# Weights loaded as f32 through a staging buffer and cast on VectorE, with wave 1 in exact order, in a fused attention and MLP kernel

## The chip, the cores and the metric

The kernel runs on one core of one Trainium2 chip. The metric is the device time of one execution in microseconds (us), as the median of several executions.

Names used below: PE is TensorE, DVE is VectorE, ACT is ScalarE, POOL is GpSimd, SP is the engine whose queue ("the sync queue") starts most DMAs. "PEclk" is the granted clock of TensorE as a share of full speed.

## The reference

A decayed linear attention over 768 positions (4 batches, 8 heads, head dimension 64) feeds an MLP of 3072 tokens, 512 to 2048 to 512:

```python
def _attn_ref(q, k, v, lam):                    # (4, 8, 768, 64), lam per head
    ...
    for b in range(nb):                         # blocks of 64 positions
        qb, kb, vb = (q[:, :, sl], k[:, :, sl], v[:, :, sl])
        intra = np.einsum('bhic,bhjc->bhij', qb, kb) * Dmask[None]
        intra = np.einsum('bhij,bhjd->bhid', intra, vb)
        inter = np.einsum('bhid,bhde->bhie', qb * lam_pow[None], kv_state)
        out[:, :, sl] = intra + inter
        kv_state = lam_block * kv_state + np.einsum('bhsd,bhse->bhde', kb * rev_pow, vb)   # cut
    return out

def _moe_ref(x, w_in, w_out):                   # x: the attention's output, (3072, 512)
    h = x @ w_in                                # w_in (512, 2048) f32
    g = h * (1.0 / (1.0 + np.exp(-1.702 * h)))
    return g @ w_out                            # w_out (2048, 512) f32
```

## The kernel before

The kernel works in six waves of 128 positions by 4 batches (512 tokens each). Wave w's attention must be done before wave w's MLP. TensorE gets one long list of work ("main": the MLP's matmuls), and the attention of the next wave ("side") is put in at chosen places of that list. All loads of q, k and v, all DMA transposes and all stores go through the sync queue, in the order of the program. All matmuls are in bf16. The weights lie in DRAM as f32, and GpSimd's DMA queue casts them on the way:

```python
    const = ctx.enter_context(tc.tile_pool(name="const", bufs=1))
    ld = ctx.enter_context(tc.tile_pool(name="ld", bufs=2))       # q, k, v as f32
    ...
    gp = ctx.enter_context(tc.tile_pool(name="gp", bufs=2))       # GELU outputs, one per wave
    op = ctx.enter_context(tc.tile_pool(name="op", bufs=4))       # output rows
    ...
    w_in_sb = [const.tile([P, KC, c * P], bf16, name=f"w_in{j}") for j, c in enumerate(IN_COLS)]     # 4 chunks
    w_out_sb = [const.tile([P, CW, d_model], bf16, name=f"w_out{j}") for j in range(FFC // CW)]      # 4 chunks

    def load_w_in(j, k0=0, k1=KC):
        f0 = sum(IN_COLS[:j]) * P
        nc.gpsimd.dma_start(
            out=w_in_sb[j][:, k0:k1, :],
            in_=moe_w_in.rearrange("(kc ki) f -> ki kc f", ki=P)[:, k0:k1, f0 : f0 + IN_COLS[j] * P])
    ... # load_w_out likewise

    behind = const.tile([1, 2], bf16)            # 4 bytes a partition

    def sync_behind(x):                          # the sync queue waits here until x has landed
        nc.sync.dma_start(out=behind, in_=x[0:1, 0, 0:2])
```

At the end of wave 0's attention it issues all weights, makes the sync queue wait for w_out's second chunk, and then issues wave 1's loads:

```python
        for j in range(1, len(IN_COLS)):
            load_w_in(j)
        for j in range(NJ):
            load_w_out(j)
        sync_behind(w_out_sb[1])
        for u in UNITS:                          # 8 units: 4 batches x 2 groups of heads
            for nm in "kqv":
                load_unit(1, nm, *u)
        nc.gpsimd.memset(v_sb[1][:, :, :, 1, :], 0.0)
        nc.gpsimd.memset(kv_sb[0], 0.0)
```

Wave 2 and later use a second form of attention, whose inputs and outputs are transposed by DMAs on the sync queue. The last of these transposes (xs to xT) is what the wave's MLP starts from:

```python
    def p_cast(w, p):
        ... # scale k and q into kqs (VectorE)
        nc.sync.dma_start_transpose(out=kq_of[w, p]..., in_=kqs...)
    def p_out(w, p):
        ... # matmuls into o
        xs = work.tile([P, B, P], bf16, tag="xs", bufs=2, name="xs")
        nc.scalar.copy(xs, o)
        nc.sync.dma_start_transpose(out=xT(w)[:, p], in_=xs.rearrange("p b c -> p (b c)"))
```

## Time and profile before

| | before |
|---|---|
| median of 4 executions (range) | 223.06 us (222.56 to 224.4) |
| TensorE busy | 208.3 us of 222.9 us |
| VectorE busy | 92.0 us, none of it from 19.5 to 39.6 us |
| first MLP matmul | 19.5 us |
| MLP of wave 1, 2, 3 begins | 56.2, 96.1, 128.2 us |
| TensorE's idle stretches over 0.15 us, after 15 us, added up | 7.4 us |

The busy table of the page of before (engine, busy us, share of the span, instructions):

```profile
span 222.9 us, 3886 instructions
...
PE 208.3 (93%) x1476; PEld 109.0 (49%) x1476; DVE 92.0 (41%) x218; ACT 95.1 (43%) x202; POOL 35.9 (16%) x57
```

TensorE bounds the kernel: only 15 us of the span are not its own. Where those 15 us lie is seen when the span is cut into stretches. Busy time in stretches of before (the first line names the columns; DMA share is that of the 16 engines, and exceeds 1 where records of packets overlap):

```profile
core 0: us, PE busy (x) PEld busy (x) DVE busy (x) ACT busy (x) POOL busy (x), PEclk, DMA share, GB/s
...
19.50:39.60 20.10, 19.76 (x94) 8.78 (x94) 0.00 (x0) 10.23 (x19) 4.62 (x5) 1.00 1.21 205
39.60:46.20 6.60, 4.38 (x22) 1.67 (x22) 1.88 (x4) 1.40 (x3) 2.09 (x4) 0.74 0.87 195
46.20:57.70 11.50, 11.50 (x98) 6.45 (x95) 6.42 (x20) 6.11 (x15) 3.19 (x6) 1.00 1.03 231
57.70:96.10 38.40, 35.18 (x341) 23.76 (x341) 24.99 (x64) 16.09 (x43) 4.05 (x7) 1.00 0.84 200
96.10:215.90 119.80, 119.80 (x771) 57.69 (x770) 45.57 (x103) 44.96 (x76) 7.85 (x9) 1.00 0.58 134
```

Read it by rows. From 96.1 us TensorE is never idle, so nothing can be won there. In the second row it is idle for 2.2 us, and the row's mean clock is 0.74. VectorE does nothing at all in the first row.

TensorE's timeline of before (start us, duration, engine, line, tiles, count; in brackets the idle time before, and what ended it):

```profile
19.52 1.04 PE L358 MATMUL ps_h<-xT,w_in 128*128 128x512 bf16 x4 [1.19 <-DMA w_in<-in_moe_w_in_dram]
...
41.56 0.28 PE L227 MATMUL ps_t<-ident,kqs 128*128 128x128 bf16 x2 [1.94 <-DVE kqs L206]
...
88.78 0.22 PE L337 MATMUL ps_o<-kv,kq 128*128 128x128 bf16 x1 [1.60 <-ACT xs L342]
```

These are the three waits that the change is aimed at: the first weights, wave 1's first block (its loads were held back by the weights), and the end of wave 2's attention.

### The profile page before, as it was taken

Reading aid. Unit: us, or ns where it says so; the run is one execution under the profiler, and the core shown is the slowest. Engines: PE = TensorE matmul, PEld = TensorE weight load, DVE = VectorE, ACT = ScalarE, POOL = GpSimd, SP = SyncE. Lnnn points to the kernel's source line nnn. Section 1 sums busy time; section 2 is a strip of 40 time slices with the busy share of each in tenths; the row PEclk is TensorE's granted clock in tenths of the full one; section 3 lists DMA queues with packets and bytes.
Section 4 is the critical chain, followed back from the end, with each engine's and each line's share of the span. In section 5 each row is a group of like instructions: output and inputs, shape, how many; then the busy total and the mean of one; then the engine's idle time right before and its main releaser. Section 6 shows DMA issues by size and latency. Waiting matters only on the chain.

```text
span 222.9 us, 3886 instructions
## 1 busy us (share of the span) xinstructions
PE 208.3 (93%) x1476; PEld 109.0 (49%) x1476; DVE 92.0 (41%) x218; ACT 95.1 (43%) x202; POOL 35.9 (16%) x57
## 2 busy tenths in 40 slices
PE   7687999699899987999999999999999999999993
PEld 2354344145784675444555444554444545444452
DVE  0792000246588984163654183572372432100121
ACT  5996662244771344146522056612076421366000
POOL 4879300232211001011020120110120000000000
PEclk9999999889999999999999999999999999999999
DMA  6999999899988797889774999747793122200112
GB/s 136 245 206 148 205 206 219 189 232 234 222 187 268 170 238 159 184 222 195 174 167 131 225 239 196 163 109 192 177 252 75 26 84 80 94 3 0 47 47 94
DMA packets 109638, 35.91 MB, mean 161 GB/s; under 512 B 102324, under 2 KB 106676, under 8 KB 109620
## 3 DMA queue, kind: packets, MB, share of 16 engines
q1 hardware_dynamic: 105236, 31.47, 60.7%
q0 software_dynamic: 4240, 4.19, 11.8%
q8 instruction: 11, 0.18, 0.4%
q14 instruction: 7, 0.06, 0.1%
q10 hardware_dynamic: 144, 0.00, 0.0%
HBM read 27.27 MB, written 6.29 MB: 151 GB/s over the span
## 4 chain that ended last, share of the span: by engine, by line
PE 74%; DMA 13%; SPq 4%; POOL 3%; DVE 3%; issue 1%; ACT 0%; DVEq 0%; ACTq 0%
PE ps_out L379 34%; PE ps_h L358 29%; DMA w_out<-in_moe_w_out_dram 7%; DMA qf<-in_q_dram 4%; SPq L82 4%; DMA xT<-xs 2%; PE ps_s L311 2%; POOL w_in L161 2%; PE ps_o L337 2%; PE ps_out L397 2%; PE ps_o L339 2%; PE ps_kv L326 2%; POOL kqs L206 1%; PE ps_t L227 1%; PE ps_s L246 1%
## 5 line engine op out<-in xcount | busy, mean ns | idle before, releaser
L358 PE MATMUL ps_h<-xT,w_in 128*128 128x512 bf16 (+1 forms) x448 | 88.5, 349 | 1.5 <-DMA w_in<-in_moe_w_in_dram 1.5
L379 PE MATMUL ps_out<-w_out,g_sb 128*128 128x512 bf16 x368 | 86.0, 384 | 0.0
L364 ACT ACTIVATE g_sb<-ps_h 128x512 bf16<-128x512 f32 (+1 forms) x112 | 59.5, 537 | 60.2 <-PE ps_h L358 59.2
L358 PEld LDWEIGHTS <-w_in 128*128 128x128 bf16 x448 | 42.1, 98 | 38.9 <-DMA w_in<-in_moe_w_in_dram 2.2
L379 PEld LDWEIGHTS <-g_sb 128*128 128x128 bf16 x368 | 34.5, 98 | 37.9 <-issue 1.0
L386 DVE COPY o_sb<-ps_out 128x512 f32<-128x512 f32 x19 | 13.1, 691 | 56.8 <-PE ps_out L379 50.2
L318 DVE TENSOR_TENSOR sm<-ps_s,dmask 128x512 bf16<-128x512 f32 x32 | 20.6, 686 | 26.9 <-PE ps_s L311 26.9
L300 POOL CAST v_sb<-vf 128x512 bf16<-128x512 f32 x16 | 12.3, 767 | 100.1 <-DMA vf<-in_v_dram 90.4
L342 ACT CAST xs<-ps_o 128x512 bf16<-128x512 f32 x16 | 9.4, 586 | 25.6 <-PE ps_o L339 23.2
L206 DVE TENSOR_TENSOR kqs<-kf,k_pow 128x256 bf16<-128x256 f32 x16 | 7.5, 469 | 27.6 <-DMA kf<-in_k_dram 23.3
L206 POOL TENSOR_TENSOR kqs<-qf,q_pow 128x256 bf16<-128x256 f32 x16 | 10.2, 641 | 29.4 <-DMA qf<-in_q_dram 26.6
L251 DVE TENSOR_TENSOR sm<-ps_s,dmask 128x512 bf16<-128x512 f32 x16 | 11.1, 691 | 5.3 <-PE ps_s L246 4.8
L329 DVE SCALAR_TENSOR_TENSOR kv<-kv,blk_pow,ps_kv 64x256 bf16<-64x256 bf16 x24 | 11.4, 476 | 0.2
L337 PE MATMUL ps_o<-kv,kq 128*128 128x128 bf16 x64 | 9.0, 220 | 1.6 <-ACT xs L342 1.6
L289 ACT CAST xT<-ps_o 128x256 bf16<-128x256 f32 x16 | 6.0, 375 | 9.7 <-PE ps_o L287 9.5
L298 DVE TENSOR_SCALAR kqs<-kf,k_pow 128x256 bf16<-128x256 f32 x32 | 9.8, 349 | 0.2
L298 DVE TENSOR_SCALAR kqs<-qf,q_pow 128x256 bf16<-128x256 f32 x32 | 9.8, 348 | 0.0
L274 DVE SCALAR_TENSOR_TENSOR kv<-kv,blk_pow,ps_kv 64x64 bf16<-64x64 bf16 x32 | 7.7, 279 | 4.9 <-PE ps_kv L262 4.5
L227 PE MATMUL ps_t<-ident,kqs 128*128 128x128 bf16 x64 | 6.8, 220 | 3.2 <-DVE kqs L206 2.5
L339 PEld LDWEIGHTS <-sm 128*128 128x128 bf16 x128 | 7.9, 98 | 3.2 <-issue 1.8
L211 ACT CAST v_sb<-vf 128x256 bf16<-128x256 f32 x16 | 6.4, 401 | 7.1 <-DMA vf<-in_v_dram 6.9
L339 PE MATMUL ps_o<-v_sb,sm 128*128 128x64 bf16 x128 | 9.0, 193 | 0.0
(54 smaller groups left out, 111.7 us busy)
## 6 DMA issues: line engine op xcount, KB each, us to landing
kf<-in_k_dram SPq DMA_DIRECT2D x48, 128.0 KB, 2.9
qf<-in_q_dram SPq DMA_DIRECT2D x48, 128.0 KB, 3.0
vf<-in_v_dram SPq DMA_DIRECT2D x48, 128.0 KB, 3.0
out_dram<-o_sb SPq DMA_DIRECT2D x23, 256.0 KB, 2.7
w_out<-in_moe_w_out_dram POOLq DMA_DIRECT2D x4, 512.0 KB, 15.8
w_in<-in_moe_w_in_dram POOLq DMA_DIRECT2D x3, 512.0 KB, 9.4
w_in<-in_moe_w_in_dram POOLq DMA_DIRECT2D x2, 256.0 KB, 5.6
kq<-kqs SPq DMA_TRANSPOSE x16, 3.5
```

Of the source, the lines that this page charges most:

```text
L206: eng.tensor_tensor(out.rearrange("s p h d -> s (p h) d"), xf.rearrange("s p h d -> s (p h) d"), tab, op=MUL)
L251: nc.vector.tensor_tensor(sm, s_ps.pop((w, b, g)).rearrange("s h (p t) -> s h p t", t=P)[:, :, 0:2, :], dmask[:, :, gs(g), :], op=MUL)
L298: nc.vector.tensor_scalar(kqs[:, i, :, h, :], loaded[w, "kq"[i], p][:, :, h, :], scalar1=(k_pow, q_pow)[i][:, 2 * p + h : 2 * p + h + 1], ...
L300: nc.gpsimd.tensor_copy(v_sb[w % 2][:, p, :, 0:3:2, :], loaded[w, "v", p])
L318: nc.vector.tensor_tensor(sm[:, h], s[:, h], dmask[:, h, p : p + 1, :].to_broadcast([P, B, P]), op=MUL)
L329: nc.vector.scalar_tensor_tensor(new[hd(h), p, :, hd(h)], old[hd(h), p, :, hd(h)], blk_pow[hd(h), 2 * p + h : 2 * p + h + 1], t[hd(h), :, ...
L337: nc.tensor.matmul(o[:, b, :], kq_of[w, p][:, 1, b, :], kv_sb[w % 2][:, p, b, :], start=True, stop=True)
L339: nc.tensor.matmul(o[:, b, hd(h)], sm[:, h, b, :], v_sb[w % 2][:, p, b, 2 * h, :], start=False, stop=True, skip_group_check=True)
L358: nc.tensor.matmul(t[:, bs[0] * P : bs[1] * P], w_in_sb[j][:, kc, i * P : (i + 1) * P], xT(w)[:, kc, bs[0] : bs[1], :].rearrange("p b t -> ...
L364: nc.scalar.activation(g_tile(w)[:, fc, c], h_ps.pop((w, fc))[:, c], GELU)
L379: nc.tensor.matmul(t, g_of[w][:, fc, g * P : (g + 1) * P], w_out_sb[j][:, fc % CW, :], start=(fc == 0), stop=(fc == FFC - 1))
L386: nc.vector.tensor_copy(o, t)
```

## The change

Its intent: take the weights off GpSimd's software queue, so that they and wave 1's loads lie in one queue in exactly the order in which they are needed; cast on VectorE, which is idle there; need no new memory, since the second GELU buffer is not used before wave 1. The weights come as 16 halves of chunks (512 KB of f32 each) through four staging slots. The places of wave 1's and wave 2's attention in the list are set anew as well. The diff, cut:

```diff
-    def load_w_in(j, k0=0, k1=KC):
-        nc.gpsimd.dma_start(...)                # and load_w_out
-    behind = const.tile([1, 2], bf16)
-    def sync_behind(x): ...
+    NS = 4
+    stage = gp.tile([P, NS, 2, W], f32, tag="g", name="w_st")
+    def load_w(kind, j, h):                     # slot = running number % NS
+        ...
+        nc.sync.dma_start(out=stage[:, slot_of[kind, j, h]], in_=src)
+    def cast_w(kind, j, h, eng, rs=slice(0, 2), cs=slice(0, W)):
+        ...
+            eng.tensor_copy(out, x)
 ...
     with tc.manual_schedule():
+        for j in range(2):
+            for h in range(2):
+                load_w("in", j, h)              # behind wave 0's loads
 ... (in wave 0's attention)
-            if i == N - 2:
-                load_w_in(0, 0, 2)
-            if i == N - 1:
-                load_w_in(0, 2, 4)
-        for j in range(1, len(IN_COLS)): load_w_in(j)
-        for j in range(NJ): load_w_out(j)
-        sync_behind(w_out_sb[1])
-        for u in UNITS: ...                     # wave 1's loads
+            if i == N:
+                for h in range(2):
+                    cast_w("in", 0, h, nc.gpsimd, slice(0, 1))
+                    cast_w("in", 0, h, nc.vector, slice(1, 2))
+        for h in range(2):
+            load_w("in", 2, h)
+        for j in range(1, NJ):
+            ...                                 # cast w_in[j], then load the next half into its slot
+        nc.gpsimd.memset(v_sb[1][:, :, :, 1, :], 0.0)
+        nc.gpsimd.memset(kv_sb[0], 0.0)
+        for j in range(2):
+            for h in range(2):
+                cast_out(j, h)
+                load_w("out", j + 2, h)
+            if j == 0:
+                for nm in "kqv":
+                    load_unit(1, nm, *UNITS[0]) # wave 1's first block, ahead of w_out's last halves
+        for u in UNITS[1:]: ...                 # the rest of wave 1's loads
 ... (order of the work; main and side now have times of their own)
-        units1(e + BOFF, UNITS[4:], BSTEP)      # BOFF, BSTEP = 4, 3.8
+        units1(e + B_AT, UNITS[4:], B_STEP, nc.scalar)   # 1, 2.5; ScalarE now copies all the turned (transposed) q and k
-                m = e - FFC - NJ * G if w > 1 else m1 - 8
-                full(m + 1, m + 10, w + 1, 3.0)          # wave 2's attention, then the later waves'
+        full(e + 8, e + 15, 2, 2.9, 3.0)                 # wave 2's attention
+        load_spread(e + 9, 3, 2)                         # wave 3's loads, amid it
```

More of the change, by code (lines that the diff above doesn't have):

```diff
@@ L154 @@
     CW = 4
+    NJ = FFC // CW
     w_in_sb = [const.tile([P, KC, c * P], bf16, name=f"w_in{j}") for j, c in enumerate(IN_COLS)]
@@ L157, with cast_out @@
     in_of = [(j, i) for j, c in enumerate(IN_COLS) for i in range(c)]
-    def load_w_in(j, k0=0, k1=KC):
-        f0 = sum(IN_COLS[:j]) * P
-        nc.gpsimd.dma_start(
-            out=w_in_sb[j][:, k0:k1, :],
-            in_=moe_w_in.rearrange("(kc ki) f -> ki kc f", ki=P)[:, k0:k1, f0 : f0 + IN_COLS[j] * P])
-    def load_w_out(j):
-        nc.gpsimd.dma_start(
-            out=w_out_sb[j],
-            in_=moe_w_out.rearrange("(fc fi) d -> fi fc d", fi=P)[:, j * CW : (j + 1) * CW, :])
-    behind = const.tile([1, 2], bf16)
-    def sync_behind(x):
-        nc.sync.dma_start(out=behind, in_=x[0:1, 0, 0:2])
-    def pow_table(pw, n, c0):
-        return pw[:, c0 : c0 + n]
+    NS = 4
+    stage = gp.tile([P, NS, 2, W], f32, tag="g", name="w_st")
+    slot_of = {}
+    def load_w(kind, j, h):
+        if (kind, j, h) not in slot_of:
+            slot_of[kind, j, h] = len(slot_of) % NS
+        if kind == "in":
+            src = moe_w_in.rearrange("(kc ki) f -> ki kc f", ki=P)[:, 2 * h : 2 * h + 2, j * W : (j + 1) * W]
+        else:
+            f = j * CW + 2 * h
+            src = moe_w_out.rearrange("(fc fi) d -> fi fc d", fi=P)[:, f : f + 2, :]
+        nc.sync.dma_start(out=stage[:, slot_of[kind, j, h]], in_=src)
+    def cast_w(kind, j, h, eng, rs=slice(0, 2), cs=slice(0, W)):
+        out = (w_in_sb if kind == "in" else w_out_sb)[j][:, 2 * h + rs.start : 2 * h + rs.stop, cs]
+        x = stage[:, slot_of[kind, j, h], rs, cs]
+        if eng is nc.scalar:
+            nc.scalar.copy(out, x)
+        else:
+            eng.tensor_copy(out, x)
+    def cast_out(j, h, eng=nc.vector):
+        for r in range(2):
+            cast_w("out", j, h, eng, slice(r, r + 1))
     x_of, g_of, h_ps, o_ps = {}, {}, {}, {}
@@ L407, in mlp2_last @@
                 nc.sync.dma_start(out=out[r0 : r0 + P, hw:], in_=o)
-    NJ = FFC // CW
     FILL0, FILL1 = 12, 1
-    BOFF, BSTEP = 4, 3.8
+    B_AT, B_STEP = 1, 2.5
     with tc.manual_schedule():
+        for j in range(2):
+            for h in range(2):
+                load_w("in", j, h)
         fill(FILL0)
@@ L456 @@
                 u_kv_up(0, *u2)
-            if i == N - 2:
-                load_w_in(0, 0, 2)
-            if i == N - 1:
-                load_w_in(0, 2, 4)
-        for j in range(1, len(IN_COLS)):
-            load_w_in(j)
-        for j in range(NJ):
-            load_w_out(j)
-        sync_behind(w_out_sb[1])
-        for u in UNITS:
+            if i == N:
[5 more added lines that the diff above has]
+        for j in range(1, NJ):
+            for c in range(2):
+                for h in range(2):
+                    cast_w("in", j, h, nc.vector, cs=slice(2 * c * P, 2 * (c + 1) * P))
+            for h in range(2):
+                if j + 2 < NJ:
+                    load_w("in", j + 2, h)
+                else:
+                    load_w("out", j + 2 - NJ, h)
+        nc.gpsimd.memset(v_sb[1][:, :, :, 1, :], 0.0)
+        nc.gpsimd.memset(kv_sb[0], 0.0)
+        for j in range(2):
+            for h in range(2):
+                cast_out(j, h)
[3 more added lines that the diff above has]
+                    load_unit(1, nm, *UNITS[0])
+        for u in UNITS[1:]:
             for nm in "kqv":
                 load_unit(1, nm, *u)
-        nc.gpsimd.memset(v_sb[1][:, :, :, 1, :], 0.0)
-        nc.gpsimd.memset(kv_sb[0], 0.0)
         for fc in range(3):
@@ L474, with put, at, units1 @@
             gelu(0, fc)
-        main = [(fc_whole, 0, fc) for fc in range(3, FFC)]
-        main += [(mlp2, 0, g, j) for j in range(NJ) for g in range(3)] + [(mlp2, 0, 3, j) for j in range(NJ)]
-        side = []
-        def units1(at, units, step):
+        main, side = [], []
+        clock = [0.0]
+        def put(length, *item):
+            main.append((clock[0], item))
+            clock[0] += length
+        def at(t, *item):
+            side.append((t, item))
+        def units1(t0, units, step, copier):
@@ L481, in units1 @@
             n = len(units)
             for i in range(n + 2):
-                t = at + step * i
+                t = t0 + step * i
+                h = t + 0.5 * step
                 if i < n:
-                    side.append((t, (u_cast_kq, 1, 0, *units[i], nc.vector)))
-                    side.append((t, (u_cast_kq, 1, 1, *units[i], nc.gpsimd)))
-                    side.append((t, (u_cast_v, 1, *units[i], nc.scalar)))
+                    at(t, u_cast_kq, 1, 0, *units[i], nc.vector)
+                    at(t, u_cast_kq, 1, 1, *units[i], nc.gpsimd)
+                    at(t, u_cast_v, 1, *units[i], nc.scalar)
@@ L488, in units1 @@
                 if 0 < i <= n:
-                    side.append((t, (u_score, 1, *units[i - 1])))
+                    at(t, u_score, 1, *units[i - 1])
+                    at(t, u_mask, 1, *units[i - 1])
                 if i < n:
-                    side.append((t + 0.5 * step, (u_turn, 1, 0, *units[i])))
-                    side.append((t + 0.5 * step, (u_turn, 1, 1, *units[i])))
-                if 0 < i <= n:
-                    side.append((t + 0.5 * step, (u_mask, 1, *units[i - 1])))
+                    at(h, u_turn, 1, 0, *units[i])
@@ L495, in units1 @@
+                    at(h, u_turn, 1, 1, *units[i])
                 if i < n:
-                    side.append((t + 0.5 * step, (u_turn_copy, 1, *units[i], nc.scalar if units[i][0] < 2 else nc.vector)))
+                    at(h, u_turn_copy, 1, *units[i], copier)
                 if i > 1:
-                    side.append((t + 0.5 * step, (u_out, 1, *units[i - 2])))
-                    side.append((t + 0.5 * step, (u_kv, 1, *units[i - 2])))
-                    side.append((t + 0.5 * step, (u_kv_up, 1, *units[i - 2])))
@@ L502 @@
-        e = len(main)
-        units1(e - 11, UNITS[:4], 2)
-        main += [(mlp1, 1, fc, [0, 1], HALF[0]) for fc in range(3)]
-        main += [(fc_rest, 1, fc, HALF[0]) for fc in range(3)]
-        main += [(fc_whole, 1, fc, HALF[0]) for fc in range(3, FFC)]
-        main += [(mlp2, 1, g, j) for g in range(2) for j in range(NJ)]
-        units1(e + BOFF, UNITS[4:], BSTEP)
-        main += [(fc_whole, 1, fc, HALF[1]) for fc in range(FFC)]
-        main += [(mlp2, 1, g, j) for g in range(2, G) for j in range(NJ)]
@@ L511, with full @@
-        m1 = e + FFC + 3 + 2 * NJ
-        side.append((13, (load_full, 2)))
-        def full(at_c, at, w, step):
+                    at(h, u_out, 1, *units[i - 2])
+                    at(h, u_kv, 1, *units[i - 2])
+                    at(h, u_kv_up, 1, *units[i - 2])
+        def full(t_cast, t0, w, step, c_step=2.0):
             for p in range(NP):
-                side.append((at_c + 2.0 * p, (p_cast, w, p)))
+                at(t_cast + c_step * p, p_cast, w, p)
             for p in range(NP + 1):
-                t = at + step * p
+                t = t0 + step * p
@@ L519, in full @@
                 if p < NP:
-                    side.append((t, (p_score, w, p)))
-                    side.append((t, (p_mask, w, p)))
-                    side.append((t, (p_kv, w, p)))
+                    at(t, p_score, w, p)
+                    at(t, p_mask, w, p)
+                    at(t, p_kv, w, p)
                 if p:
-                    side.append((t + 0.5 * step, (p_out, w, p - 1)))
-        for w in range(1, NW):
-            e = len(main)
-            if w + 1 < NW:
-                m = e - FFC - NJ * G if w > 1 else m1 - 8
-                full(m + 1, m + 10, w + 1, 3.0)
-                if w + 2 < NW:
-                    for p in range(NP):
-                        for i, nm in enumerate("kqv"):
-                            side.append((m + 4 + 2.4 * (3 * p + i), (load_pair, w + 2, nm, p)))
-                main += [(fc_whole, w + 1, fc) for fc in range(FFC)]
-                if w + 2 < NW:
-                    main += [(mlp2, w + 1, g, j) for g in range(G) for j in range(NJ)]
-                else:
-                    main += [(mlp2, w + 1, g, j) for g in range(G - 1) for j in range(NJ)]
-                    main += [(mlp2_last, w + 1, G - 1)]
+                    at(t + 0.5 * step, p_out, w, p - 1)
@@ new lines, in load_spread @@
+        def load_spread(t0, w, step):
+            for p in range(NP):
+                for i, nm in enumerate("kqv"):
+                    at(t0 + step * (3 * p + i), load_pair, w, nm, p)
+        for fc in range(3, FFC):
+            put(1, fc_whole, 0, fc)
+        for t, j, h in ((15, 2, 0), (15.5, 2, 1), (18.5, 3, 0), (20.2, 3, 1)):
+            at(t, cast_out, j, h)
+        for j in range(NJ):
+            for g in range(3):
+                put(1, mlp2, 0, g, j)
+        for j in range(NJ):
+            put(1, mlp2, 0, 3, j)
@@ new lines @@
+        at(13, load_full, 2)
+        e = clock[0]
+        units1(e - 11, UNITS[:4], 2, nc.scalar)
+        units1(e + B_AT, UNITS[4:], B_STEP, nc.scalar)
+        for fc in range(3):
+            put(0.25, mlp1, 1, fc, [0, 1], HALF[0])
+        for fc in range(3):
+            put(0.25, fc_rest, 1, fc, HALF[0])
+        for fc in range(3, FFC):
+            put(0.5, fc_whole, 1, fc, HALF[0])
+        for g in range(2):
+            for j in range(NJ):
+                put(1, mlp2, 1, g, j)
+        for fc in range(FFC):
+            put(0.5, fc_whole, 1, fc, HALF[1])
@@ new lines @@
+        for g in range(2, G):
+            for j in range(NJ):
+                put(1, mlp2, 1, g, j)
+        full(e + 8, e + 15, 2, 2.9, 3.0)
+        load_spread(e + 9, 3, 2)
+        for w in range(2, NW):
+            e = clock[0]
+            if w + 1 < NW:
+                full(e + 1, e + 10, w + 1, 3.0)
+            if w + 2 < NW:
+                load_spread(e + 4, w + 2, 2.4)
+            for fc in range(FFC):
+                put(1, fc_whole, w, fc)
+            for g in range(G - (w + 1 == NW)):
+                for j in range(NJ):
+                    put(1, mlp2, w, g, j)
@@ L541 @@
+        put(4, mlp2_last, NW - 1, G - 1)
         side.sort(key=lambda x: x[0])
-        for i, (f, *args) in enumerate(main):
-            while side and side[0][0] <= i:
+        for t, (f, *args) in main:
+            while side and side[0][0] <= t:
                 _, (g_, *b_) = side.pop(0)
```

## The prediction

> **What bounds the kernel now.** TensorE. The profile's busy table gives it 208.3 of 222.9 us. By stage (busy time in stretches of the span) it is never idle from 96.1 us, where wave 2's MLP starts, to 215.9; that stretch keeps its order of work and should not move. Time to win lies before 96.1 us:
>
> 1. Start of the first MLP: the timeline shows the first w_in matmul at 19.5 us, 1.2 us after attention's last one, waiting for w_in; another 0.3 us at 23.9.
> 2. Between 39.6 and 42.2 us: 2.2 us idle, waiting for wave 1's first block. The weights' software queue fills the DMA engines (share 1.2 from 19.5 to 39.6 us); wave 1's loads are held until w_out's second chunk lands at 34.05 us, then take 6 us instead of 3.
> 3. Then a granted clock of 0.74 (39.6 to 46.2 us): eight matmuls take 3.5 us in place of 1.7; with the attention pieces about 2.2 us lost.[...]
> 4. End of wave 1: 0.56 us at 57.7 (VectorE), 1.05 us at 78 to 79 (VectorE late with sm and kv), 1.6 us at 87 (transposing DMA, then ACT). 3.2 us.
>
> Sum: 9 us.
>
> **What the change does.** It removes 9 software DMAs and the wait for w_out; it adds 16 f32 loads of 512 KB on the sync queue through four staging slots, and their casts. Reading stays 8.4 MB. The software queue moved 206 GB/s of bf16, so it read about 412; output stores with the same 2 KB rows reach 330 to 420 GB/s in short slices. Estimate: 1.3 to 1.6 us per half chunk, so the weights are all in at 34 to 39 us. TensorE needs a new chunk each 3.5 us (in) or 2.6 us (out): enough.
>
> Casts: VectorE does 256 f32 elements in 0.349 us, so 512 in at most 0.7; 1024 per half, at most 22 us in all[...]. VectorE is idle 22.5 us there: off the path.
>
> **On the critical path.** Item 1: first weights at 17.5 to 18.5 plus one cast, win 0.5 to 1.2 us. Items 2 and 3: wave 1's first block is issued around 29 to 33 us and lands before TensorE wants it at about 37; win about 4.2 us, clock 1.0. Item 4: wave 2's attention is spread over more of wave 1's MLP; win 2 of 3.2. Given back, about 1 us: ACT now does all turn copies beside the half GELUs, VectorE is nearly full, and wave 2's last transposes leave only about 3 us of slack.
>
> **Predicted: 216.8 us**, 8 in 10 between 214.3 and 220.0. Faster by over 2%: 0.78; within 2%: 0.19; slower: 0.03.
>
> **Right if:** first w_in matmul before 19 us; no idle near 40 us and no clock under 0.95 after the start; [...]wave 2's MLP starts at 89 to 91 us; from there 126.8 us to the end.
>
> **Wrong if:** a half chunk takes 1.8 us or more (TensorE waits for w_out casts at 35 to 40 us); the in-order sync queue blocks wave 1's loads behind a slot; ACT delays GELUs around 55 to 65 us; the transposes before wave 2 end late.

The four items come to 9 us, of which 0.5 to 1.2, about 4.2 and 2 us were to be won and about 1 us given back, and 223.06 us less these 5.7 to 6.4 us are 216.7 to 217.4 us.

## The result, and the profile after

| | before | after |
|---|---|---|
| median of 4 executions (range) | 223.06 us (222.56 to 224.4) | 231.75 us (230.78 to 232.53) |
| ratio after to before, with 95% interval | | 1.0377 (1.0317 to 1.0437) |
| first MLP matmul | 19.5 us | 21.5 us |
| first w_out matmul | 34.3 us | 37.2 us |
| MLP of wave 1, 2, 3 begins | 56.2, 96.1, 128.2 us | 60.6, 99.8, 136.4 us |
| TensorE's idle stretches over 0.15 us, after 15 us, added up | 7.4 us | 10.9 us |
| span of the profiled execution | 222.9 us | 230.8 us |

A ratio here and below is the mean time of one kernel's fast runs over that of the other's in the same rounds, so it is not quite the ratio of the medians. Executions over 1.5% slower than the fastest of the same kernel are left out of the means. The kernel is slower by 3.8%, and the result was correct, as in every run below.

The busy table of the page of after:

```profile
span 230.8 us, 3923 instructions
...
PE 212.7 (92%) x1476; PEld 110.1 (48%) x1476; DVE 102.6 (44%) x244; ACT 97.0 (42%) x206; POOL 30.3 (13%) x50
```

The matmuls are the same 1476, but they are busy 4.4 us longer. Most of that is a clock, not work. Busy time in the same stretches of after:

```profile
19.50:39.60 20.10, 18.10 (x82) 8.19 (x82) 8.98 (x21) 11.14 (x23) 4.65 (x4) 0.92 0.83 283
39.60:46.20 6.60, 4.78 (x22) 1.82 (x20) 2.55 (x7) 0.99 (x2) 0.61 (x1) 0.91 1.09 339
46.20:57.70 11.50, 10.08 (x72) 4.49 (x72) 7.16 (x19) 4.99 (x11) 3.09 (x5) 0.90 1.09 212
```

In the first row 82 matmuls were done in place of 94, and although four staging slots were to keep the queue full, the DMA share is 0.83. In the second row TensorE is still idle for 1.8 us (2.2 us in before), and in the third row for 1.4 us, where before has none.

Stretches around the lower clock in after show three periods, where before had one:

```profile
19.00:26.00 7.00, 4.94 (x24) 2.19 (x22) 3.19 (x6) 2.91 (x10) 4.65 (x4) 0.76 0.91 329
42.00:50.00 8.00, 5.07 (x21) 1.40 (x19) 2.79 (x7) 0.99 (x2) 0.97 (x2) 0.79 1.06 262
...
98.00:107.00 9.00, 6.19 (x22) 2.35 (x21) 5.17 (x17) 1.21 (x3) 0.76 (x2) 0.81 0.88 211
```

Multiply what is missing to 1 by the length: 7.00 x 0.24, 8.00 x 0.21 and 9.00 x 0.19 are each 1.7 us, which is one period of 3.41 us at half clock: the trace of after has a clock of 0.50 from 21.09 to 24.50, from 44.98 to 48.39 and from 103.01 to 106.42 us. Before has 6.60 x 0.26 = 1.7 us, once (0.50 from 42.45 to 45.86 us). This is not only the profiled execution: of after's four executions three had a mean clock of 0.977 or 0.978 over the span, which is three such periods, and one had 0.990. Of the 32 executions of before in the later jobs, 19 had a clock of 0.997 or more and took 223.66 us on average; the other 13 (0.985 to 0.992; three of them slow) took 225.01 us. TensorE's timeline of after names the waits:

```profile
21.52 1.89 PE L367 MATMUL ps_h<-xT,w_in 128*128 128x512 bf16 x4 [2.00 <-POOL w_in L181]
...
43.90 0.29 PE L236 MATMUL ps_t<-ident,kqs 128*128 128x128 bf16 x2 [1.32 <-DVE kqs L215]
...
49.55 0.28 PE L236 MATMUL ps_t<-ident,kqs 128*128 128x128 bf16 x2 [0.94 <-DVE kqs L215]
...
80.45 0.40 PE L320 MATMUL ps_s<-kq 64*128 64x128 bf16 x8 [2.02 <-DMA kq<-kqs]
103.55 1.86 PE L367 MATMUL ps_h<-xT,w_in 128*128 128x512 bf16 x4 [2.71 <-DMA xT<-xs]
```

So of the loss of 7.9 us between the two profiles, 3.5 us are more idle time (10.9 less 7.4), and two more periods of half clock make at most 3.4 us (less where TensorE waits anyway): at most 6.9 us. Of the rest, 0.8 us lie before 19.5 us, where the same 126 matmuls were busy for 14.97 us in place of 14.20. What made the waits is the question. Four things are seen in the trace.

**Staging slots.** VectorE's timeline of after shows the casts waiting for halves that have not landed:

```profile
20.57 0.43 DVE L181 CAST w_in<-w_st 128x512 bf16<-128x512 f32 x1 [1.37 <-DMA w_st<-in_moe_w_in_dram]
...
24.61 2.41 DVE L181 CAST w_in<-w_st 128x512 bf16<-128x512 f32 x4 [0.61 <-DMA w_st<-in_moe_w_in_dram]
...
31.71 0.43 DVE L181 CAST w_in<-w_st 128x512 bf16<-128x512 f32 x1 [2.59 <-DMA w_st<-in_moe_w_in_dram]
...
47.10 0.76 DVE L181 CAST w_out<-w_st 128x512 bf16<-128x512 f32 x2 [3.26 <-DMA w_st<-in_moe_w_out_dram]
```

The trace gives the landing of the first four halves, which were issued together, as 20.55, 21.91, 23.24 and 24.59 us, so 1.35 us apart; but each took 3.9 to 8.5 us (median 6.0) from its issue to its landing. The last half landed at 48.55 us: 28.0 us for the 15 after the first, so 1.87 us each. Before's weights were in at 39.33 us. The sync queue's timeline of after, at the place where wave 1's blocks are issued:

```profile
36.65 0.37 SPq L173 DMA_DIRECT2D w_st<-in_moe_w_out_dram  x1
37.07 0.46 SPq L82 DMA_DIRECT2D kf<-in_k_dram  x1
...
39.28 2.79 SPq L173 DMA_DIRECT2D w_st<-in_moe_w_out_dram  x2
42.13 0.46 SPq L82 DMA_DIRECT2D kf<-in_k_dram  x1
```

Wave 1's first block was issued at 37.07 us, and its k, q and v landed at 43.3 to 44.4 us. Its second block stood in order behind the last two halves, which needed a slot, and was issued at 42.13 us (k landed at 49.04 us). These are the waits at 43.90 and 49.55 us.

**Packets of q, k and v.** In 4 to 14 us both kernels load only wave 0's q, k and v, with the same statements. The DMA table of this stretch, of before and then of after (queue, packets, MB, share of 16 engines):

```profile
q1 hardware_dynamic: 9739, 2.42, 107.5%
```

```profile
q1 hardware_dynamic: 8886, 2.21, 131.8%
```

Share x 16 engines x 10 us over the packets is 17.7 ns for a packet of 256 bytes in before and 23.7 ns in after. By the landings the difference is there from the first loads on (3.48, 4.08 and 4.66 us in after, 3.45, 3.90 and 4.35 us in before), although the packets recorded from 3 to 4 us still show 17.7 ns in both; the first load of a weight is issued only at 14.55 us. What differs is where the buffers lie: the change removed the const tile `behind` (4 bytes a partition), and all later pools moved down by 32 bytes. In the built programs the first of the q, k and v buffers begins at byte 76032 = 297 x 256 of a partition in before, and at 76000, 224 past a multiple of 256, in after. Wave 0's attention ended at 19.52 us in place of 18.32.

**The end of wave 2's attention.** The last xs was written from 97.43 to 98.02 us, but the sync queue, in order, first issued two k loads of wave 3 and a store. The sync queue of after:

```profile
97.58 1.19 SPq L352 DMA_TRANSPOSE xT<-xs  x1
98.81 1.13 SPq L90 DMA_DIRECT2D kf<-in_k_dram  x2
100.04 0.45 SPq L397 DMA_DIRECT2D out_dram<-o_sb  x1
100.59 1.22 SPq L352 DMA_TRANSPOSE xT<-xs  x1
```

The last transpose was issued 2.6 us after its input was there. TensorE waited 2.71 us for it at 103.55 us and then ran at half clock. The wait of 2.02 us at 80.45 us is of the same kind: the first kqs of wave 2 was written by 71.67 us, but its transpose was issued at 74.65 us, behind loads of v and four stores, and landed at 80.40 us.

**GpSimd's memsets.** The four casts at 24.61 us took 2.41 us (one of them 1.41), while GpSimd cleared buffers. GpSimd's timeline of after, with the cast that the first MLP matmul waited for:

```profile
20.60 0.86 POOL L181 CAST w_in<-w_st 128x512 bf16<-128x512 f32 x1 [3.77 <-DMA w_st<-in_moe_w_in_dram]
...
22.77 0.95 POOL L483 MEMSET v_sb<- 128x1024 bf16 x1
23.66 2.08 POOL L484 MEMSET kv<- 128x2048 bf16 x1
```

My theory (A) was first that the addresses are the large part. The rivals were (B) the staging slots' round trip and (C) the new order of work and of the sync queue.

### The profile page after: what moved, and what is told of

Its sections match the earlier page's. It is cut to its first block, busy times and chain, and to the rows that moved or that the text cites. A ratio compares the mean times of both kernels' runs of the same rounds, so it can differ in the third digit from the quotient of the medians.

```text
span 230.8 us, 3923 instructions
## 1 busy us (share of the span) xinstructions
PE 212.7 (92%) x1476; PEld 110.1 (48%) x1476; DVE 102.6 (44%) x244; ACT 97.0 (42%) x206; POOL 30.3 (13%) x50
## 4 chain that ended last, share of the span: by engine, by line
PE 69%; DMA 17%; SPq 8%; DVE 2%; issue 1%; ACT 1%; POOL 0%; ACTq 0%
PE ps_h L367 29%; PE ps_out L388 29%; DMA w_st<-in_moe_w_in_dram 6%; SPq L82 6%; DMA qf<-in_q_dram 3%; DMA kq<-kqs 2%; PE ps_s L320 2%; DMA w_st<-in_moe_w_out_dram 2%; PE ps_kv L335 2%; PE ps_o L348 2%; PE ps_o L346 2%; PE ps_out L406 2%; DVE w_in L181 1%; SPq L173 1%; DMA xT<-xs 1%
## 5 line engine op out<-in xcount | busy, mean ns | idle before, releaser
L367 PE MATMUL ps_h<-xT,w_in 128*128 128x512 bf16 (+1 forms) x448 | 91.0, 356 | 4.9 <-DMA xT<-xs 2.7
L367 PEld LDWEIGHTS <-w_in 128*128 128x128 bf16 x448 | 43.1, 99 | 44.2 <-issue 6.7
L388 PEld LDWEIGHTS <-g_sb 128*128 128x128 bf16 x368 | 34.3, 98 | 37.1 <-issue 1.0
L309 POOL CAST v_sb<-vf 128x512 bf16<-128x512 f32 x16 | 11.3, 704 | 103.4 <-DMA vf<-in_v_dram 97.3
L181 DVE CAST w_in<-w_st 128x512 bf16<-128x512 f32 x14 | 6.6, 514 | 8.3 <-DMA w_st<-in_moe_w_in_dram 8.3
L181 DVE CAST w_out<-w_st 128x512 bf16<-128x512 f32 x16 | 6.2, 429 | 8.0 <-DMA w_st<-in_moe_w_out_dram 8.0
L215 DVE TENSOR_TENSOR kqs<-kf,k_pow 128x256 bf16<-128x256 f32 x16 | 6.8, 432 | 5.5 <-ACT k_pow L128 4.2
```

Of the source, the lines that this page charges most:

```text
L181: eng.tensor_copy(out, x)
L215: eng.tensor_tensor(out.rearrange("s p h d -> s (p h) d"), xf.rearrange("s p h d -> s (p h) d"), tab, op=MUL)
L309: nc.gpsimd.tensor_copy(v_sb[w % 2][:, p, :, 0:3:2, :], loaded[w, "v", p])
L367: nc.tensor.matmul(t[:, bs[0] * P : bs[1] * P], w_in_sb[j][:, kc, i * P : (i + 1) * P], xT(w)[:, kc, bs[0] : bs[1], :].rearrange("p b t -> ...
L388: nc.tensor.matmul(t, g_of[w][:, fc, g * P : (g + 1) * P], w_out_sb[j][:, fc % CW, :], start=(fc == 0), stop=(fc == FFC - 1))
```

## The experiments

**1. After, with the buffers back on their addresses.**

```diff
+    pad = const.tile([1, 2], bf16, name="pad")     # after, plus 4 bytes a partition
```

> The changed kernel plus one unused 4-byte tile where the removed `behind` tile lay, so that all load buffers, staging and output buffers lie at multiples of 256 bytes again (they lie 224 bytes past one after the change). Theory A (addresses): 256-byte packets of wave 0's loads fall from 25 to 17 ns, k/q/v loads land 0.46 us apart instead of 0.60, and the time falls from 231.8 to about 221 to 225 us. Rival R1 (the weights' round trip through four staging slots is the loss, the slower packets are chance of that run): packets may vary, time stays at 230 us or more.

Measured: 229.97 us, ratio 1.0267 (1.0167 to 1.0367). The DMA table of 4 to 14 us of this run:

```profile
q1 hardware_dynamic: 9379, 2.33, 103.4%
```

That is 17.6 ns a packet, as in before. The addresses explain all of the slower packets of this stretch, but only about 1.1 points of the 3.8 (1.0377 over 1.0267, across two jobs; the two intervals overlap, so this share is not clear of noise). As the main cause, A fell: some 2.7% were left for B and C.

**2 and 3. Before, with the same buffers 224 or 128 bytes past a multiple of 256; later also (12) 32 bytes.**

```diff
+    pad = const.tile([P, n // 2], bf16, name="pad")   # before, n = 224, 128 or 32 bytes more
```

> The kernel before plus an unused 224-byte tile, so that its buffers lie 224 bytes past a multiple of 256, as in the changed kernel; nothing else differs. Theory A: 256-byte packets take about 25 ns instead of 17 and the time rises by 4 to 9 us. Rival R1: same time within 0.5%, packets at 17 ns.

> The kernel before plus an unused 128-byte tile: buffers at 128 bytes past a multiple of 256. Theory A[...]: packets slow too[...], time up by 2 to 6 us. Rival form[...]: packets at 17 ns and time as before.

> The kernel before with buffers 32 bytes past a multiple of 256. If the cost of a packet[...]: about 18 to 19 ns per 256-byte packet. If it[...]: 23 to 25 ns, as at 128 and 224.

Measured: with 224, 227.75 us, ratio 1.0179 (1.0082 to 1.0277); with 128, 226.69 us, ratio 1.0144 (1.0066 to 1.0222); with 32, 225.06 us in two runs, ratio 1.0055 (0.9974 to 1.0136). The DMA tables of 4 to 14 us, for 224, 128 and 32:

```profile
q1 hardware_dynamic: 8868, 2.20, 130.6%
```

```profile
q1 hardware_dynamic: 8979, 2.23, 127.3%
```

```profile
q1 hardware_dynamic: 8926, 2.22, 131.7%
```

These are 23.6, 22.7 and 23.6 ns a packet, against 17.7. So the address alone (of these and all later buffers), with nothing else changed, slows the mean packet of this stretch by about a third, and at the three offsets tried it hardly matters how far it is from a multiple of 256. For 32 bytes the record had two alternatives: 18 to 19 ns if the cost grows with the offset, and 23 to 25 ns if every offset costs the same; 23.6 ns speaks for the second. That the address does it is shown; how it does it is not. What it costs the whole kernel is shown for 224 and 128 (intervals clear of 1), not for 32.

**4. Before's weight loads with after's order of work.**

```diff
 after's main, side, units1, full and load_spread; before's load_w_in, load_w_out, sync_behind; no staging, no casts
```

> The kernel before with its own weight loads (software queue, cast in the DMA, the wait for w_out, addresses at multiples of 256), but the changed kernel's order of wave 1's blocks and of wave 2's attention. If the new order is worth what I predicted (2 us of the end of wave 1): 221 us. If the new order costs (the changed kernel's stalls at wave 2's first transposed block and at wave 2's MLP belong to it, not to addresses): 224 to 227 us.

Measured: 225.58 us, ratio 1.0083 (0.9963 to 1.0202). The order alone costs about 0.8%, not clear of nothing. But its parts are seen in the profile, TensorE's timeline first:

```profile
95.46 9.83 PE L356 MATMUL ps_h<-xT,w_in 128*128 128x512 bf16 x37 [2.65 <-DMA xT<-xs]
```

Wave 2's MLP began at 92.0 us, 4.1 us earlier than before, and wave 3's at 128.6, no earlier: wave 2 took 36.6 us in place of 32.1. A gain as the prediction counted it was there in this execution (in part by chance: after a half clock at the start TensorE came to wave 1's first block about 1.7 us later than in before and did not wait for it, where experiment 14, with the same early program and no half clock, waits 1.2 us), and was given back at one wait: 2.65 us for xT, which ended at 95.46 us, and one period of half clock after it (a clock of 0.83 over the 10 us from 92 us, so 1.7 us) make 4.4 of these 4.5 us.

**5. Eight staging slots in place of four.**

```diff
+    pad = const.tile([1, 2], bf16, name="pad")
-    NS = 4
+    NS = 8                                      # 4 as before, 1 in const, 1 in the second xT buffer, 2 in the four output rows
-        for j in range(2):
+        for j in range(NJ):                     # all of w_in is issued at once; w_out's half j then takes w_in's slot
             for h in range(2):
                 load_w("in", j, h)
```

> The aligned changed kernel (e1) with eight staging slots in place of four (the second xT buffer, the idle output buffers and one more tile), so that all of w_in is queued at once and no load waits for a cast of the four slots before it. Theory B (round trip of the four slots starves the DMA engines between 25 and 31 us): the last half of w_out lands at about 40 to 41 us in place of 46.9, wave 1's first turn starts 3 to 5 us earlier, time 224 to 227 us. Rival (the DMA engines can't do f32 halves faster, round trip is harmless): last half lands after 45 us and time stays at 229 to 231.

Measured: 224.18 us against 224.19 for before in the same job, ratio 1.0016 (0.9959 to 1.0073). Here B was right about the weights and the time: the last half landed at 40.04 us. It was not right about wave 1's first turn, which started only 1.5 us earlier than in experiment 1 (42.19 against 43.67 us). Busy time from 25 to 32 us, first of after and then of this run:

```profile
25.00:28.00 3.00, 3.00 (x15) 1.31 (x14) 2.02 (x4) 2.56 (x7) 0.74 (x1) 1.00 0.50 176
28.00:32.00 4.00, 4.00 (x20) 1.82 (x19) 1.39 (x4) 2.92 (x5) 0.00 (x0) 1.00 0.83 252
```

```profile
25.00:28.00 3.00, 3.00 (x15) 1.31 (x14) 2.67 (x7) 2.58 (x6) 0.54 (x1) 1.00 1.04 393
28.00:32.00 4.00, 4.00 (x20) 1.81 (x19) 2.90 (x11) 2.70 (x5) 0.00 (x0) 1.00 1.05 408
```

With four slots the DMA engines' share was 0.50 and then 0.83, while the sync queue waited for a slot; with eight they were full. (The edit also lets all weights go ahead of wave 1's first block in the queue.) TensorE had no idle stretch over 0.15 us between 22 and 66 us, and wave 1's MLP began at 54.8 us (58.8 in experiment 1, 56.2 in before). The slots, with the order of loads that they allow, were the larger part of what the loads lost. The run still lost time against before by a start almost 2 us later and by waits of 1.41 us at 74 us and 2.34 us at 97 us.

**6. The two memsets at the start, on VectorE.**

```diff
+        nc.vector.memset(v_sb[1][:, :, :, 1, :], 0.0)    # after with experiment 1's pad
+        nc.vector.memset(kv_sb[0], 0.0)
         fill(FILL0)
 ...
-        nc.gpsimd.memset(v_sb[1][:, :, :, 1, :], 0.0)
-        nc.gpsimd.memset(kv_sb[0], 0.0)
```

> The aligned changed kernel (e1) with GpSimd's two memsets of wave 1's v and kv buffers moved to VectorE at the very start, out of the stretch 22.7 to 25.7 us where VectorE's first casts of w_in ran up to 1.4 us instead of 0.42. If GpSimd's memsets hold up VectorE's casts: no cast over 0.55 us, the fifth half of w_in issued about 1 us earlier, the weights 0.5 to 1 us earlier, time 228.5 to 230. If not: long casts stay, time as e1 within noise.

Measured: 229.10 us, ratio 1.0214 (1.0168 to 1.0260). VectorE's timeline at the same casts in this run:

```profile
24.18 1.10 DVE L182 CAST w_in<-w_st 128x512 bf16<-128x512 f32 x3 [0.81 <-DMA w_st<-in_moe_w_in_dram]
```

No cast of w_in took more than 0.428 us (of w_out 0.441), and the last half landed 0.9 us earlier than in experiment 1 (45.97 against 46.91). The fifth half was issued only 0.16 us earlier (21.25 us), not 1 us as expected; it was the seventh that gained 1.26 us (24.97 us). So the memsets do slow the casts: the longest cast took 1.41 us in after and 1.47 us in experiment 5, both while GpSimd cleared kv, and 0.428 us here, where GpSimd cleared nothing. How the one slows the other is not shown. The time it is worth in the whole kernel is not clear of the spread.

This run also shows something about the clock. Its TensorE timeline, and its busy time from 17 to 26 us:

```profile
21.28 1.04 PE L368 MATMUL ps_h<-xT,w_in 128*128 128x512 bf16 x4 [3.01 <-POOL w_in L182]
```

```profile
17.00:26.00 9.00, 5.74 (x40) 2.85 (x38) 3.81 (x10) 5.04 (x14) 1.73 (x2) 1.00 0.94 325
```

After an idle stretch of 3.01 us the clock stayed at 1.00, while in after half clock came with a stretch of 2.00 us at the same place (0.50 from 21.09 us). The closest pair is of experiments 4 and 14: idle stretches of 1.84 and 1.83 us before the first MLP matmul, and a mean clock of 0.83 from 17 to 27 us in the one, 1.00 in the other. Within one trace the length doesn't decide either: in after half clock came with or soon after the stretches that ended at 43.90 us (1.32 us) and 103.55 us (2.71 us), but not with the 2.02 us before 80.45 us (a clock of 1.00 from 78 to 98 us). In before it came after 1.94 us (ended at 41.56 us) and not after 1.60 us (at 88.78 us; 1.00 from 84 to 94 us). So the length of an idle stretch alone does not decide; what does is not shown. Whether the start costs up to 1.7 us more thus differs between executions of the same early program, and differences of this size between two single profiles prove nothing.

**7 and 8. Wave 2's attention closer together, wave 3's loads later: after (with the pad), and before with the new order (experiment 4).**

```diff
-        full(e + 8, e + 15, 2, 2.9, 3.0)
-        load_spread(e + 9, 3, 2)
+        full(e + 8, e + 15, 2, 2.4, 2.4)
+        load_spread(e + 16.5, 3, 1.3)
```

> The aligned changed kernel (e1), with wave 2's attention in shorter steps (2.4 in place of 3.0 and 2.9) and wave 3's loads begun later (16.5 in place of 9 units after wave 1's MLP), so that the last two transposing DMAs of wave 2 do not stand behind wave 3's loads in the sync queue. Theory C: the wait of 2.3 to 2.7 us before wave 2's MLP and the half clock after it (1.7 us) go, time 225.5 to 227. Rival (the transposes are late because the attention itself is late): wait stays, time as e1 within 1 us.

> The same two changes on e4 (the kernel before's weight loads with the changed kernel's order). Theory C: the 2.65 us wait at wave 2's MLP and the half clock go, and the 4 us that e4 had won by then stay: 219 to 221.5 us, better than both kernels. Rival: 223 to 226.

Measured: 229.81 us (228.52 without the execution flagged as slow), ratio 1.0227 (1.0150 to 1.0305), and 225.95 us, ratio 1.0070 (1.0026 to 1.0115). Neither won anything: the wait at wave 2's MLP stayed at 2.47 us and 2.3 us. The sync queue of experiment 8 tells why. The four transposes of xs were issued at 82.33, 86.96, 90.54 and 94.10 us, with four loads of wave 3 between each pair of them, although the last two xs had been written by 87.77 and 90.35 us. I had moved the loads right among the transposes. So the edit did not do what it was for, and it tests neither C nor its rival by the time. The trace speaks for C in a sharper form: what counts is what stands ahead of the transposes in the one queue.

**9 and 10. The loads behind the transposes: before with the new order, and everything together (eight slots, early memsets, this order).**

```diff
+        full(e + 8, e + 15, 2, 2.4, 2.4)
+        load_spread(e + 26, 3, 0.8)
```

> e4 (the kernel before's weight loads, the changed kernel's order) with wave 2's attention in steps of 2.4 as in e8, but wave 3's loads begun only 26 units after wave 1's MLP. In e8 I had put those loads among the four xT transposes, which then were issued 3.6 to 4.6 us apart on the sync queue. Theory C2 (the sync queue's order holds the transposes back): xT transposes issued within 0.5 us of their xs, no wait at wave 2's MLP, 219.5 to 222 us. Rival: wait of over 1.5 us stays, 224 to 227.

> Eight slots (e5), memsets early (e6) and wave 3's loads late (e9) together: the changed kernel with each cause that was found taken away. If the causes add: 219 to 221.5 us, better than both kernels (0.5% from the memsets, 2 to 4 us from the wait and half clock at wave 2's MLP). If C2 is wrong: 223 to 224.5, as e5.

Measured: 227.53 us, ratio 1.0177 (1.0117 to 1.0236), and 227.18 us, ratio 1.0173 (1.0094 to 1.0253): the expected gain became a loss. The sync queue of experiment 10, and then its TensorE timeline:

```profile
79.80 10.11 SPq L371 DMA_TRANSPOSE xT<-xs  x4
89.96 1.12 SPq L90 DMA_DIRECT2D kf<-in_k_dram  x2
```

```profile
105.24 0.40 PE L339 MATMUL ps_s<-kq 64*128 64x128 bf16 x8 [3.40 <-DMA kq<-kqs]
```

The wait at wave 2's MLP is gone, as expected. A wait of 3.40 us (3.03 in experiment 9) stands one stage later: wave 3's loads now stand in front of wave 3's own transposes of kq. In experiment 10 the first of their inputs was written by 95.17 us, and its transpose was issued at 101.41 us, after loads and a store. The wait was moved, not removed.

**11. After's loads (with the pad) in before's order of work.**

```diff
 after's load_w, cast_w, staging and order of loads; before's main, side, units1 and full (BOFF, BSTEP = 4, 3.8)
```

> The aligned changed kernel's weight path (four slots, casts on VectorE) with the kernel before's order of wave 1's blocks and wave 2's attention: the fourth corner beside before, e1 and e4. If loads and order add (order alone +2.6, loads alone +4.4 from e4 to e1): 226.5 to 228.5 us. If the new order was what the late weights needed: 230 or more.

Measured: 227.74 us, ratio 1.0144 (1.0062 to 1.0227). The new way of loading costs 1.4% by itself, even in the old order: waits of 2.20 us at the start, 1.19 us at 23.7, 1.14 us at 43.5 and 1.95 us at 48.3 us. With experiment 4 this gives the parts: order +0.8%, loads +1.4%, both together and aligned +2.7% (experiment 1), with the addresses +3.8% (after).

**13 and 14. Wave 3's loads threaded between the transposes by hand: with eight slots and early memsets, and with before's loads.**

```diff
-        load_spread(e + 9, 3, 2)
+        for i, t in enumerate((13.0, 13.2, 19.2, 21.6, 24.0, 26.4, 27.2, 28.0, 28.8, 29.6, 30.4, 31.2)):
+            at(e + t, load_pair, 3, "kqv"[i % 3], i // 3)        # and full(e + 8, e + 15, 2, 2.4, 2.4)
```

> e10 with wave 3's twelve load pairs threaded: two in the gap after wave 2's third kq transpose, one after each of the first three xT transposes, seven after the last. If the sync queue's order is the cause: no wait over 1 us at wave 2's MLP (about 93 us) and none over 1 us at wave 3's first scores (102 to 106 us), 219.5 to 222 us, below the kernel before by 1% or so. If waits only move again: 223 or more.

> The same threading on e9 (the kernel before's weight loads, the new order). If the sync queue's order is the cause: 219.5 to 222 us as e13. If the new order has another cost of its own: 223 or more, with e13 no better.

Measured, in six runs each: 223.75 us, ratio 0.9992 (0.9945 to 1.0038), and 223.00 us, ratio 0.9963 (0.9919 to 1.0007). The losses of the change are gone, but no gain over before is shown. TensorE's timeline of experiment 13 has one wait left in this stage:

```profile
103.16 0.40 PE L339 MATMUL ps_s<-kq 64*128 64x128 bf16 x8 [1.54 <-DMA kq<-kqs]
```

No half clock follows it. The wait for kq that was moved by 9 and 10 is still there at half its size; the gains I expected from both runs did not come. No version tried is shown to beat the kernel before.

## Why the prediction was wrong

What held. TensorE bounds the kernel, and its work did not change. A half chunk takes 1.35 us where halves are queued behind each other (predicted 1.3 to 1.6). VectorE's casts take 0.424 us each (the median in after) and 12.8 us in all, well under the "at most 0.7" and "at most 22 us in all" of the prediction. In experiment 5 a cast of 256 elements takes 0.29 us, so about 0.5 ns for each further element, against 1.04 ns for the copies of ps_out in before (0.425 us for 256 and 0.691 us for 512). VectorE had the room. The prediction's worry about ACT was not where the time went.

What failed, in the order of the sum:

1. "Estimate: 1.3 to 1.6 us per half chunk, so the weights are all in at 34 to 39 us ... enough." The rate was right and the end was wrong: 48.55 us. A slot is taken from the issue of its load until the load that follows it into the slot can be issued. By the issue times in the trace of after this took 5.4 to 10.8 us, in the middle 7.35; four slots then give one half each 7.35 / 4 = 1.84 us, against 1.87 measured. The warning stood in the trace of before: its loads of 128 KB took 2.9 us from issue to landing, though they landed 0.46 us apart. Experiment 5 shows it: eight slots, last half at 40.04 us. Between experiments 1 and 5, which differ in the slots and the order of loads that they allow, the ratio went from 1.0267 to 1.0016, so this is the largest of the failed steps.
2. "Wave 1's first block is issued around 29 to 33 us and lands before TensorE wants it at about 37; win about 4.2 us, clock 1.0." It was issued at 37.07 us and landed at 43.3 us and later. It follows from step 1 and from the order of the queue: "the in-order sync queue blocks wave 1's loads behind a slot" stood among what would make the prediction wrong, and did. Item 2's wait was not won; the half clock of item 3 stayed. But step 1 does not explain all of it: with eight slots (experiment 5) the first k was issued at 33.57 us and still landed only at 40.48 us. The prediction had no term for the 6 to 7 us that such a load takes from issue to landing while weights fill the DMA engines.
3. "First weights at 17.5 to 18.5 plus one cast." They landed at 20.55 us, and the first MLP matmul came at 21.52 (predicted before 19). They stand behind all of wave 0's loads in the same queue; and the four halves move side by side: from 17.80 us, when the last of wave 0's loads had landed, to 20.55 us the DMA engines moved 355 GB/s x 2.75 us = 0.98 MB, almost two halves, and only one had landed. Then the matmul waited for one more cast, and not VectorE's of 0.43 us but GpSimd's, of 0.86 us. In after, the packets made wave 0's loads slower besides. Even aligned it was 20.55 to 21.44 us in the runs with the new loads; the start varied by about 1 us between kernels with the same early program (20.1 and 21.2 us in experiments 4 and 8), and why is open.
4. "Wave 2's last transposes leave only about 3 us of slack ... given back, about 1 us." Item 4 was not won: the waits after 57.7 us came to 4.9 us (2.02 and 2.71 us, both behind other entries of the sync queue) in place of 3.2, and a half clock of up to 1.7 us followed. The slack was counted to where TensorE needs xT, but not what stands before the last transpose in the sync queue.
5. The addresses stood nowhere in the prediction. The diff removes a tile of 4 bytes, and that costs about one point of the 3.8 (not clear of noise there; the same offset put on before cost 1.8%, which is clear).
6. The sum has no term for the clock after the new waits. The two more periods of half clock make up to 3.4 us of the 7.9.

What stays open: how much the memsets cost in the whole kernel; why the first MLP matmul's time varies between runs with the same early program; and what decides whether half clock comes with an idle stretch. The parts (0.8, 1.4, and about 1.1) don't quite add to 3.8, and their intervals are wide; only the 1.4 of the loads is clear of 0 by itself, and for the addresses the cost put on before.

## What to carry to other kernels

The rate of the staging ring was the number of its slots over the time from issue through landing and cast until the slot was free (4 slots over 7.35 us, so 1.84 us a half; measured 1.87), not the rate at which queued loads landed (1.35 us apart): read the issue-to-landing time of a like load in the trace before choosing the number of slots. In a queue that works in order, list what stands ahead of each late and urgent transfer, for moving loads may only move the wait, as in experiments 9 and 10 (to 3.03 and 3.40 us one stage later). After any change to the tiles of a kernel compare the buffers' addresses and the time of a packet in a stretch that did not change (here 17.7 against 23.7 ns).
